# Three-stage float32 kernel: the order of its instructions as lists instead of a planner

## The chip, the cores and the metric

The kernel runs on one core of one Trainium2 chip. The metric is the device time of one execution in microseconds (us); lower is better. The engines are called as the profile calls them: PE is TensorE's matmul, PEld its weight load, DVE is VectorE, ACT is ScalarE, POOL is GpSimd, SP is SyncE, whose queue issues nearly all DMAs.

## The reference

Three stages in float32. A delta-rule attention over 4 batches, 8 heads, 768 steps of 48 features; then a feed-forward layer with squared relu (384 to 2048 to 384); then one whose hidden layer is the maximum of three products (384 to 768 to 384). The 3072 rows are the 4 x 768 tokens.

```python
def _attn_ref(q, k, v, beta):
    k_n = k / (np.linalg.norm(k, axis=-1, keepdims=True) + 1e-06)
    for t in range(S):
        kt, vt, bt = (k_n[:, :, t], v[:, :, t], beta[:, :, t, None])
        y[:, :, t] = np.einsum('bhd,bhde->bhe', q[:, :, t], state)
        v_old = np.einsum('bhde,bhd->bhe', state, kt)
        state = state + bt[:, :, :, None] * np.einsum('bhd,bhe->bhde', kt, vt - v_old)

def _moe_ref(x, w_in, w_out):
    r = np.maximum(x @ w_in, 0.0)
    return (r * r) @ w_out

def _moe2_ref(x, w1, w2, w3, w_out):
    return np.maximum(np.maximum(x @ w1, x @ w2), x @ w3) @ w_out
```

## The kernel before

The tokens are cut into six blocks of 128 steps (index t), 512 tokens each over the four batches. The attention of a block is done in chunks of 64 steps. `gram` (L593) transposes k and q and multiplies keys with keys and queries; `solve` (L687) inverts the small triangular systems, with nearly a hundred short DVE instructions on the tiles `L`, `T`, `F`, `step` and `tmp`, a transposition `L<-G` ahead of them and the transpositions `Tn<-T` and `G<-T` behind them, and small PE products (`Tn,G`, `G`, `G,L`, `L,Tn`); `chain` (L789) carries the state from chunk to chunk, with small PE products (`US,W`, `R,G`, `US,kn`, `W,US`), and leaves the block's output in `xr`. `split` (L922) makes a high and a low part of it, `xh` and `xl`, on ACT and DVE.

The first feed-forward layer (`moe1`, L968) takes a block in 16 slices f of 128 hidden features. `hidden` makes nine matmuls of 512 columns (three of 128 rows each, for three products of high and low parts), three ACT passes (`r`, `r`, `gh`) and one DVE pass (`gl`); `project` makes nine matmuls more with the weights `wo`. In the first block eight slices are done in two halves of 256 columns (`HALF`), and each slice's weights are made there, out of raw float32 words, into a high and a low part: two steps on `word` and `raw` on ACT, four on DVE, and one more on each for the parts (`wih`, `wil` or `wo`). They are written to a DRAM copy (`wod`), from which later blocks load them. The third stage (`maxout`, L1125, and `project2`, L1142) comes at the end, when the first one's outputs of all blocks are there.

All small products are float32 matmuls of 64 columns or fewer; all large ones have 256 to 512 columns and operands in the faster type `F32R`. PE changes between the two kinds: a row of small products is put between rows of large ones.

No engine call goes straight into the program. `_Engine.__getattr__` (L322) records it; `together` (L78) binds calls into one step; `issue` (L292) puts the steps of one of three parts of the kernel into an order and makes the calls, and each engine runs its instructions in that order. The waits between engines are put in by the layer below, from the tiles that the instructions read and write. The order is the `Planner`'s (L54): `add` (L84) notes each step's cost and which steps it depends on, `forward` (L120) lists them by due time on five modelled engines, `backward` (L248) makes new due times out of the result, eight rounds in all, and the best is kept. The due times that it starts from are set along the code in `pl.at`, from constants such as `GL`, `CL`, `GRAM`, `SOLVE` and `CHAIN`; `MIX`, `FULL`, `STAY` and others steer when PE changes kind.

Of the kernel before, what the change touches and what calls it, by code (L numbers as in the profile page):

```python
# [17 lines left out]
WINDOW = 10.24 / 3  # L18
ROUNDS = 8


def _row(t):
    n = 1
    for x in t.shape[1:]:
        n *= x
    return n


def _region(ap):

    t, dims = ap.tensor, list(ap.ap)
    if "DRam" in type(t).__name__:
        return None
    if ap.space == DRAM:
        tile_size = t.shape[-2] * t.shape[-1]
        n = ap.size() // tile_size
        return t.name, 0, 128, ((1 << n) - 1) << (ap.offset // tile_size)
    row = _row(t)
    p0, off = divmod(ap.offset, row)
    if ap.space == PSUM:  # L40
        return t.name, 0, 128, -1
    off += sum(step * (n - 1) for step, n in dims[1:] if step < 0)
    bits = 1
    for step, n in sorted((abs(step), n) for step, n in dims[1:]):
        if step:
            out, done = 0, 0
            while done < n:
                out |= bits << (step * done)
                done += 1
            bits = out  # L50
    return t.name, p0, p0 + (dims[0][0] // row) * (dims[0][1] - 1) + 1, bits << off


class Planner:  # L54

    MIX, FULL, STAY, BURST, URGENT = 0.01, 0.27, 35.22, 19.14, -2.36
    INTO, BACK, RUSH = 0.12, 0.24, 4.896
    HOLD = {"vector": 0.198, "sync": 38.55}
    CHUNK, SUPPLY, AHEAD = 256, 4.0, 128
    EVENT, LANES = 0.065, 8
    PHASE = 67
    LAG = {"tensor": 0.2, "vector": 0.13, "scalar": 0.15, "gpsimd": 0.08, "sync": 0.0}

    def __init__(self, nc):
        self.nc, self.at, self.ops, self.seen, self.joint, self.beside = nc, 0.0, [], {}, None, False  # L70
        self.free, self.first, self.end, self.before_all, self.rush = {}, 0, {}, False, False
        self.flow, self.ticks, self.start = (deque(), False, False, (self.PHASE, -9.0, False)), {}, {}
        self.marks = {}, {}, {}, {}
# [4 lines left out]
    def together(self, beside=False):  # L78

        self.joint, self.beside = len(self.ops), beside  # L80
        yield
        self.joint, self.beside = None, False

    def add(self, engine, call, cost, outs, ins, flow, late, count=0):  # L84
        if self.joint is None or self.joint == len(self.ops):
            self.ops.append([engine, [], 0.0, set(), self.at, any(a.dtype == F32R for a in ins), 0.0, 0.0, self.before_all, self.rush, 0])
        n = len(self.ops) - 1
        op = self.ops[n]
        op[1].append(call)
        op[10] += count  # L90
        op[2] = max(op[2], cost) if self.beside else op[2] + cost
        op[6] += flow
        op[7] = late
        for write, aps in ((False, ins), (True, outs)):
            for ap in aps:
                region = _region(ap)
                if region is None:
                    continue
                name, p0, p1, bits = region
                kept = []  # L100
                for e in self.seen.get(name, ()):
                    m, w, a0, a1, b = e
                    other = bits < 0 and self.ops[m][0] != engine
                    if (write or w or other) and a0 < p1 and p0 < a1 and b & bits:
                        if m != n:
                            op[3].add(m)
                        if write and p0 <= a0 and a1 <= p1 and not b & ~bits:
                            continue
                    kept.append(e)
                kept.append((n, write, p0, p1, bits))  # L110
                self.seen[name] = kept

    def lag(self, m, n):

        e, f = self.ops[m][0], self.ops[n][0]
        if f == "tensor":
            return 0.0 if e == "tensor" else self.LAG[e] + 0.1
        return self.LAG[e]

    def forward(self, at):  # L120

        first, ops = self.first, self.ops
        free, ticks, flow, fill, big, (count, since, thin) = dict(self.free), dict(self.ticks), *self.flow
        flow = deque(flow)
        known, snaps, place, count_of = self.marks
        known, snaps = {e: dict(k) for e, k in known.items()}, {e: list(x) for e, x in snaps.items()}
        place, count_of = dict(place), dict(count_of)
        left, ready, queue, seq = {}, {}, {}, []
        start, end = {}, self.end
        end = dict(end)  # L130
        for n in range(first, len(ops)):
            left[n] = len(self.before[n])

        def there(n):
            t = 0.0
            for m in ops[n][3]:
                t = max(t, end[m] + self.lag(m, n))
            heappush(ready.setdefault(ops[n][0], []), (t, n))

        for n in range(first, len(ops)):  # L140
            if not left[n]:
                there(n)
        todo = len(ops) - first
        while todo:
            best = None
            for e in self.LAG:
                f = free.get(e, 0.0)
                if queue.get(e):
                    t = f
                elif ready.get(e):  # L150
                    t = max(f, ready[e][0][0])
                else:
                    continue
                if best is None or t < best[0]:
                    best = t, e
            t, e = best
            q = queue.setdefault(e, [])
            r = ready.get(e, [])
            hold, later = self.HOLD.get(e, 0.0), []
            while r and r[0][0] <= t + (max(self.RUSH, hold) if hold else 0.0):  # L160
                when, n = heappop(r)
                if when <= t + hold or ops[n][9]:
                    heappush(q, (at[n], n))
                    start[n] = when
                else:
                    later.append((when, n))
            for x in later:
                heappush(r, x)
            n = q[0][1]
            if e == "tensor":  # L170
                while flow and flow[0][0] < t - WINDOW:
                    flow.popleft()
                load = sum(x[1] for x in flow)
                fill = load < (self.FULL if fill else self.MIX)
                kinds = [min((x for x in q if ops[x[1]][5] == f), default=None) for f in (False, True)]
                used = count % self.CHUNK - self.CHUNK * (t - since) / self.SUPPLY
                thin = used > (0 if thin else self.AHEAD)
                if None not in kinds:
                    if fill or thin:
                        n = kinds[True][1]  # L180
                    else:
                        lead = kinds[True][0] - kinds[False][0]
                        if not big:
                            stay = lead > -self.STAY
                        else:
                            stay = lead < self.URGENT and sum(
                                ops[x[1]][2] for x in q if not ops[x[1]][5]
                            ) < self.BURST
                        n = kinds[big if stay else not big][1]
            q.remove((at[n], n))  # L190
            heapify(q)
            t = start[n] = max(t, start[n])
            seq.append(n)
            cost = ops[n][2]
            k, need = known.setdefault(e, {}), {}
            for m in ops[n][3]:
                f, p = ops[m][0], place[m]
                if f == e == "tensor":
                    continue
                r, p = (p % self.LANES, p // self.LANES + 1) if f == "sync" else (f, p)  # L200
                if p > k.get(r, 0):
                    need[r] = max(p, need.get(r, 0))
            for r, p in need.items():
                k[r] = max(p, k.get(r, 0))
                if r != e and r in snaps:
                    for x, y in snaps[r][p - 1].items():
                        k[x] = max(y, k.get(x, 0))
# [40 lines left out]
    def backward(self, end):  # L248
# [5 lines left out]
        def there(n):  # L254
            t = 0.0
# [950 lines left out]
```

## Time and profile before

| | us |
|---|---|
| median of 3 runs | 900.05 (893.88 to 901.16) |
| profiled execution | 900.32 |
| its span, first to last instruction | 898.6 |
| PE busy | 849.2 |
| DVE busy | 550.0 |
| ACT busy | 458.6 |
| POOL busy | 34.6 |

The profile is one execution, with every instruction of every engine. Spans of matmuls overlap, so a PE that is busy all the time may still run at different rates; the count of matmuls in a stretch tells more. The granted clock is a share of PE's full speed. All recorded calls have one line in the profile, L371, so instructions are told apart by operation, tiles and shape.

### The profile page before, as it was taken

The page shows a single profiled execution, that of the slowest core. Times are in us where ns is not written, and L with a number is a line of the kernel's source. Part 1 is how long each engine was busy: PE and PEld are TensorE (multiplying, and loading weights), DVE is VectorE, ACT ScalarE, POOL GpSimd, SP SyncE. Part 2 cuts the span into 40 slices and gives each one's busy share as a digit, 9 for nine tenths or more (in the row PEclk, how much of TensorE's full clock was granted, in tenths as well). Part 3 has the DMA queues.
Part 4 walks back from the last instruction along what each step waited for, and adds up shares of the span by engine and source line. Part 5 has one row for each costly group of instructions (what it writes and reads, how often), then busy time and mean ns, then how long its engine had stood idle before and what let it go on. Part 6 is the DMA issues. An engine that isn't in the chain of part 4 may idle for free.

```text
span 898.6 us, 24256 instructions
## 1 busy us (share of the span) xinstructions
PE 849.2 (95%) x10284; PEld 716.3 (80%) x10284; DVE 550.0 (61%) x1325; ACT 458.6 (51%) x876; POOL 34.6 (4%) x55
## 2 busy tenths in 40 slices
PE   4558999999989999999999999999999999999998
PEld 4447987778768787878878888888888889898987
DVE  5999989879769869969742999223324141413131
ACT  6557877974755575574555899432212121212111
POOL 6000001000100000000000000000000000000000
PEclk9556999999999999999999999999999999999999
DMA  8854584764377466544234777320100000000000
GB/s 209 188 141 110 149 288 124 182 152 129 49 151 176 82 125 144 140 92 109 89 104 138 229 259 232 106 88 1 53 18 37 35 1 36 1 35 1 29 8 36
DMA packets 166893, 96.06 MB, mean 107 GB/s; under 512 B 130560, under 2 KB 146816, under 8 KB 166784
## 3 DMA queue, kind: packets, MB, share of 16 engines
q1 hardware_dynamic: 166272, 94.40, 39.1%
q8 instruction: 81, 1.33, 0.6%
q14 instruction: 28, 0.23, 0.1%
q0 software_dynamic: 512, 0.10, 0.1%
HBM read 79.53 MB, written 14.94 MB: 105 GB/s over the span
## 4 chain that ended last, share of the span: by engine, by line
PE 87%; DVE 5%; ACT 3%; DMA 3%; issue 1%; ACTq 0%; DVEq 0%
PE ps L371 87%; DMA raw<-in_moe_w_in_dram 2%; DVE word L371 1%; DVE T L371 1%; DVE step L371 1%; ACT W L371 1%; ACT G L371 1%; DMA raw<-in_moe_w_out_dram 1%; DVE W L371 1%; DVE F L371 0%; ACT word L371 0%; DVE tmp L371 0%; DMA wo<-wod 0%; ACT US L371 0%; DVE wil L371 0%
## 5 line engine op out<-in xcount | busy, mean ns | idle before, releaser
L371 DVE TENSOR_TENSOR r<-r,ps 128x512 f32<-128x512 f32 x72 | 49.5, 688 | 178.0 <-PE ps L371 176.0
L371 PE MATMUL ps<-gh,wo 128*128 128x512 f32 (+1 forms) x624 | 156.9, 378 | 1.3 <-DMA wo<-wod 0.7
L371 ACT ACTIVATE r<-ps 128x512 f32<-128x512 f32 (+1 forms) x140 | 80.0, 571 | 139.1 <-PE ps L371 132.6
L371 PEld LDWEIGHTS ps<-gh,wo 128*128 128x128 f32 x624 | 110.4, 188 | 22.5 <-DMA wo<-wod 1.1
L371 PE MATMUL ps<-xh,wih 128*128 128x512 f32 (+1 forms) x312 | 120.8, 387 | 0.5 <-ACT r L371 0.5
L371 PE MATMUL ps<-xh,wil 128*128 128x512 f32 (+1 forms) x312 | 117.2, 376 | 0.0
L371 PE MATMUL ps<-xl,wih 128*128 128x512 f32 (+1 forms) x312 | 117.1, 375 | 0.0
L371 DVE TENSOR_TENSOR gl<-r,gh 128x512 fp32r<-128x512 f32 (+1 forms) x104 | 67.3, 647 | 60.1 <-ACT gh L371 55.7
L371 PE MATMUL ps<-gl,wo 128*128 128x512 f32 (+1 forms) x312 | 84.2, 379 | 0.0
L371 PEld LDWEIGHTS ps<-xh,wih 128*128 128x128 f32 x312 | 59.3, 190 | 12.1 <-ACT r L371 0.7
L371 PEld LDWEIGHTS ps<-xl,wih 128*128 128x128 f32 x312 | 59.2, 190 | 10.8
L371 PEld LDWEIGHTS ps<-xh,wil 128*128 128x128 f32 x312 | 59.4, 190 | 9.5
L371 PEld LDWEIGHTS ps<-gl,wo 128*128 128x128 f32 x312 | 56.2, 190 | 11.0 <-DVE gl L371 0.4
L371 ACT ACTIVATE gh<-r 128x512 fp32r<-128x512 f32 (+1 forms) x104 | 62.0, 596 | 3.3 <-PE ps L371 1.3
L371 ACT ACTIVATE r<-r 128x512 f32<-128x512 f32 (+1 forms) x104 | 62.0, 597 | 2.4
L371 ACT ACTIVATE G<-ps 32x256 f32<-32x256 f32 (+3 forms) x116 | 50.3, 448 | 19.0 <-PE ps L371 17.5
L371 PE MATMUL ps<-W 64*64 64x64 f32 (+1 forms) x1664 | 41.2, 244 | 10.1 <-ACT W L371 7.1
L371 PEld LDWEIGHTS ps<-W 64*64 64x64 f32 (+1 forms) x1664 | 35.9, 151 | 17.7 <-ACT W L371 9.1
L371 DVE TENSOR_SCALAR word<-word 128x384 f32<-128x384 f32 (+1 forms) x112 | 41.1, 369 | 9.2 <-ACT word L371 7.9
L371 ACT ACTIVATE m0h<-r 128x512 fp32r<-128x512 f32 x18 | 11.4, 632 | 67.2 <-DVE r L371 67.2
L371 ACT ACTIVATE m1h<-r 128x512 fp32r<-128x512 f32 x18 | 11.4, 632 | 66.6 <-DVE r L371 66.6
L371 ACT ACTIVATE ob<-ps 128x384 f32<-128x384 f32 x24 | 11.8, 491 | 58.3 <-PE ps L371 58.3
(155 smaller groups left out, 1775.1 us busy)
## 6 DMA issues: line engine op xcount, KB each, us to landing
wo<-wod SPq DMA_DIRECT2D x88, 384.0 KB, 3.5
raw<-in_moe_w_out_dram SPq DMA_DIRECT2D x22, 384.0 KB, 4.0
raw<-in_moe_w_dram SPq DMA_DIRECT2D x18, 384.0 KB, 3.6
raw<-in_moe_w_in_dram SPq DMA_DIRECT2D x16, 384.0 KB, 3.8
wod<-wo SPq DMA_DIRECT2D x16, 384.0 KB, 4.5
out_dram<-ob SPq DMA_DIRECT2D x24, 192.0 KB, 1.8
x2d<-raw SPq DMA_DIRECT2D x12, 256.0 KB, 3.5
vn<-in_v_dram SPq DMA_DIRECT2D x14, 192.0 KB, 4.4
```

The source lines that it names most:

```text
L371: self.plan.add(self.name, lambda: fn(*args, **kw), cost, [out], ins, flow, late, count)
```

## The change

The planner, its costs and all due times are gone. A `Recorder` keeps only the recorded calls, in the order in which the code makes them, bound by `together` as before; `ORDER` has three lists of numbers, one for each part, and `issue` makes the calls in their order. The numbers come from a search outside the kernel that moved steps about in each engine's order. The code that makes the calls is the same but for the removed due times, so the steps and their tiles are the same; ACT's program has one more table load.

```diff
-class Planner:
...
-    MIX, FULL, STAY, BURST, URGENT = 0.01, 0.27, 35.22, 19.14, -2.36
...
+ORDER = [
+    """
+30 7 0 27 25 1 24 26 31 5 1096 2 3 1112 15 35 36 1128 37 38 167 49 22 39 50 51 20 52 40 6 53 41 21 42 43 1097 44 45
...
+class Recorder:
+    def __init__(self, nc):
+        self.nc, self.ops, self.joint, self.part = nc, [], None, 0
...
+    def add(self, call):
+        if self.joint is None or self.joint == len(self.ops):
             self.ops.append([])
+        self.ops[-1].append(call)

     def issue(self):
...
-        for k in range(ROUNDS):
-            plan = self.forward(at)
...
-            at = self.backward(plan[2])
...
+        order = [int(n) for n in ORDER[self.part].split()]
+        assert sorted(order) == list(range(len(self.ops)))
+        for n in order:
+            for call in self.ops[n]:
                 call()
+        self.ops, self.part = [], self.part + 1
...
-    GL, CL, G1, DEC, BOOST, SPL, CUT, HALF, G2, LATE, BLOCKS, FIRST, HURRY = -882, 745, 733, 1375, 2244, -595, 6, 8, -527, 228, 3, 0, 0
...
+    CUT, HALF, BLOCKS = 6, 8, 3
```

ACT at the start of the program. `tmp<-ident` is a square root of one element that loads the table with the square root; `word` and `raw` belong to the first weights. Before:

```order
L371 ACT_TABLE_LOAD
L371 ACTIVATE tmp<-ident 128x1
L371 ACTIVATE word_84<-raw_81 128x384
L371 ACTIVATE raw_81<-raw_81 128x384
```

And now, where `tmp<-ident` stands; `st<-st` is the first solve's square root, `W_105` and `G_107` are the first block's keys and products:

```order
L258 ACTIVATE wo_98<-word_84 128x384
L258 ACTIVATE G_107<-ps_93 128x512
L258 ACTIVATE W_105<-ps_90 64x8x64 x2
L258 ACTIVATE word_85<-raw_81 128x384
L258 ACT_TABLE_LOAD
L258 ACTIVATE tmp<-ident 128x1
L258 ACTIVATE st<-st 128x32
```

The one-element square root moved from ACT's first place to behind the first block's evictions. A table load still stands first on ACT, in front of `W_105<-ps_86`, and a second one stands here.

DVE in the first half block of the first feed-forward layer, from the first `gl` to the second `gl`. `L`, `T`, `F`, `step` and `tmp` are those of the second block's solve (t = 1); `F<-F,step` is its first half, `step<-T,F` and `T<-T,step` its second. Before:

```order
L371 TENSOR_TENSOR gl_79<-r_75,gh_77 128x256
L371 TENSOR_TENSOR T<-T,tmp 128x2x4x12
L371 TENSOR_TENSOR step_121<-L,T 128x192
L371 TENSOR_TENSOR tmp<-L,T 128x78
L371 TENSOR_TENSOR F<-F,step_121 128x16x12
L371 TENSOR_TENSOR T<-T,tmp 128x2x3x13
L371 TENSOR_TENSOR step_120<-L,T 128x208
L371 TENSOR_TENSOR F<-F,step_120 128x16x13
L371 TENSOR_TENSOR xl<-xr,xh 128x4x64 x3
L371 TENSOR_TENSOR tmp<-L,T 128x56
L371 TENSOR_TENSOR gl_80<-r_76,gh_78 128x256
L371 TENSOR_TENSOR wo_98<-word_84,wo_98 128x384
```

And now:

```order
L258 TENSOR_TENSOR F<-F,step_121 128x256
L258 TENSOR_TENSOR gl_79<-r_75,gh_77 128x256
L258 TENSOR_TENSOR step_120<-T,F 128x240
L258 TENSOR_TENSOR step_121<-T,F 128x224
L258 TENSOR_TENSOR T<-T,F 128x16x16
L258 TENSOR_TENSOR xl<-xr,xh 128x4x64 x2
L258 TENSOR_TENSOR T<-T,step_120 128x15x16
L258 TENSOR_TENSOR wo_98<-word_84,wo_98 128x384
L258 TENSOR_TENSOR step_120<-T,F 128x208
L258 TENSOR_TENSOR T<-T,step_121 128x14x16
L258 TENSOR_TENSOR gl_80<-r_76,gh_78 128x256
```

The solve has moved forward past the first block's slices: its first half, which was still under way at the first `gl`, is now over there, and its second half stands among the first `gl` and `wo`.

PE where the second block's solve is used. `Tn,G_108`, `G_108`, `G_108,L` and `L,Tn` are its small products, the rest are large matmuls of `hidden` and `project`. Before, in the first block's slices of 512 columns:

```order
L371 MATMUL ps_90<-Tn,G_108 32x32
L371 MATMUL ps_90<-G_108 32x32
L371 MATMUL ps_88<-gh_77,wo_100 128x512 x2
L371 MATMUL ps_86<-gl_79,wo_100 128x512
L371 MATMUL ps_87<-gl_79,wo_100 128x512
L371 MATMUL ps_88<-gl_79,wo_100 128x512
L371 MATMUL ps_86<-gh_78,wo_101 128x512 x2
L371 MATMUL ps_87<-gh_78,wo_101 128x512 x2
L371 MATMUL ps_91<-G_108,L 32x32
L371 MATMUL ps_90<-L,Tn 32x32
```

And now, where the last half slice ends (the pieces of 4x64 columns):

```order
L258 MATMUL ps_90<-Tn,G_108 32x32
L258 MATMUL ps_90<-G_108 32x32
L258 MATMUL ps_89<-xh,wih 128x512
L258 MATMUL ps_89<-xh,wil 128x512
L258 MATMUL ps_89<-xl,wih 128x512
L258 MATMUL ps_86<-gl_80,wo_101 128x4x64
L258 MATMUL ps_87<-gl_80,wo_101 128x4x64
L258 MATMUL ps_88<-gl_80,wo_101 128x4x64
L258 MATMUL ps_86<-gh_77,wo_98 128x512 x2
L258 MATMUL ps_90<-Tn,G_108 32x32
L258 MATMUL ps_90<-G_108 32x32
```

The products of one solve stood in two rows of 64, with nine large matmuls between them. Now the first 64 are in three parts of 32, 16 and 16, with two and eight large ones between these, and 16 large ones stand before the other 64; all of it comes earlier among the large matmuls.

## Rows read from the trace of the kernel before

**Rows 1.** The page: busy time by engine, PE in 40 slices, the instruction queue's packets

```profile
PE 849.2 (95%) x10284; PEld 716.3 (80%) x10284; DVE 550.0 (61%) x1325; ACT 458.6 (51%) x876; POOL 34.6 (4%) x55
...
PE   4558999999989999999999999999999999999998
...
q8 instruction: 81, 1.33, 0.6%
```

**Rows 2.** Stretches: us, busy us (count) of PE, PEld, DVE, ACT, POOL; clock; DMA

```profile
30.00:90.00 60.00, 34.88 (x968) 30.13 (x964) 57.71 (x191) 36.78 (x76) 3.15 (x4) 0.57 0.55 138
...
91.00:150.00 59.00, 57.86 (x712) 52.83 (x702) 55.53 (x154) 47.30 (x109) 1.36 (x2) 1.00 0.63 200
...
100.00:130.00 30.00, 28.88 (x287) 28.11 (x287) 26.98 (x73) 23.67 (x62) 0.00 (x0) 1.00 0.82 269
...
150.00:160.00 10.00, 8.14 (x231) 6.66 (x217) 8.42 (x16) 7.38 (x14) 1.99 (x2) 0.83 0.39 101
...
150.00:190.00 40.00, 36.78 (x1060) 29.13 (x1050) 31.35 (x60) 34.67 (x73) 3.96 (x6) 0.96 0.64 156
...
200.00:220.00 20.00, 20.00 (x90) 16.57 (x89) 19.69 (x82) 9.32 (x15) 0.00 (x0) 1.00 0.47 148
...
245.00:275.00 30.00, 27.21 (x758) 21.34 (x758) 21.39 (x59) 15.00 (x33) 0.00 (x0) 0.94 0.74 144
...
275.00:425.00 150.00, 148.44 (x2729) 120.83 (x2728) 127.77 (x338) 90.16 (x164) 6.34 (x8) 1.00 0.54 124
...
314.38:331.65 17.27, 17.27 (x435) 14.01 (x429) 10.68 (x15) 13.29 (x27) 1.90 (x2) 1.00 0.61 118
...
485.00:895.00 410.00, 410.00 (x1969) 351.97 (x1967) 158.87 (x278) 148.77 (x274) 0.00 (x0) 1.00 0.20 67
```

**Rows 3.** PE's waits by releaser (us, times, longest): from 120 us on; 150 to 190

```profile
PE ps L371 <- issue: 6.7, 6, 1.9
...
PE ps L371 <- issue: 3.0, 2, 1.9
```

**Rows 4.** PE, instructions in order of time (start, us; idle before in brackets), 147 to 262

```profile
147.15 0.73 PE L371 MATMUL ps<-gh,wo 128*128 128x512 f32 x2
...
149.41 0.21 PE L371 MATMUL ps<-G,L 32*32 32x32 f32 x1
...
152.06 0.21 PE L371 MATMUL ps<-G,L 32*32 32x32 f32 x1 [1.86 <-issue]
...
154.08 0.63 PE L371 MATMUL ps<-xl,wih 128*128 128x512 f32 x1
154.51 0.63 PE L371 MATMUL ps<-xh,wih 128*128 128x512 f32 x1
...
261.28 0.34 PE L371 MATMUL ps<-US,W 64*64 64x48 f32 x2 [1.95 <-issue]
```

**Rows 5.** ACT, PE and DVE in order of time, up to 21 us

```profile
0.81 1.28 ACT L371 ACT_TABLE_LOAD   x1 [0.81 <-PEq L1190]
2.10 0.20 ACT L371 ACTIVATE tmp<-ident 128x1 f32<-128x1 f32 x1
...
7.58 1.09 PE L371 MATMUL ps<-ident,kt 128*128 128x128 f32 x4 [7.58 <-DMA kt<-in_k_dram]
...
5.01 0.76 DVE L371 TENSOR_SCALAR word<-word 128x384 f32<-128x384 f32 x2 [2.94 <-ACT word L371]
...
18.47 1.95 DVE L371 STREAM_TRANSPOSE L<-G 128x1024 f32<-128x1024 f32 x1
```

**Rows 6.** DVE and PE in order of time: a first solve's step, the eighth `gl`, a transposition

```profile
45.82 0.40 DVE L371 TENSOR_TENSOR step<-T,F 128x240 f32<-128x240 f32 x1
...
109.38 0.42 DVE L371 TENSOR_TENSOR gl<-r,gh 128x256 fp32r<-128x256 f32 x1
...
111.94 0.28 PE L371 MATMUL ps<-gl,wo 128*128 128x256 f32 x1
...
143.31 2.04 DVE L371 STREAM_TRANSPOSE G<-T 128x1024 f32<-128x1024 f32 x1
```

More of the change, by code (lines that the diff above doesn't have):

```diff
@@ L17 @@
 DRAM = bass.MemoryType.DRAM
[L18 to L51, printed above, removed]
-class Planner:
-    MIX, FULL, STAY, BURST, URGENT = 0.01, 0.27, 35.22, 19.14, -2.36
[L62 to L67, printed above, removed]
+ORDER = [
+    """
[148 rows of a table added]
+""",
+    """
[22 rows of a table added]
+""",
+    """
[22 rows of a table added]
+""",
+]
+class Recorder:
     def __init__(self, nc):
[L70 to L73, printed above, removed]
+        self.nc, self.ops, self.joint, self.part = nc, [], None, 0
         for name in ("tensor", "vector", "scalar", "gpsimd", "sync"):
@@ L77, in together @@
     @contextmanager
-    def together(self, beside=False):
-        self.joint, self.beside = len(self.ops), beside
+    def together(self):
+        self.joint = len(self.ops)
         yield
-        self.joint, self.beside = None, False
-    def add(self, engine, call, cost, outs, ins, flow, late, count=0):
+        self.joint = None
+    def add(self, call):
         if self.joint is None or self.joint == len(self.ops):
[L86 to L207, printed above, removed]
-            place[n] = count_of.get(e, 0) + (e != "sync")
-            count_of[e] = count_of.get(e, 0) + 1
-            if e != "sync":
-                snaps.setdefault(e, []).append(dict(k))
-            if e in ("vector", "scalar"):
-                cost += self.EVENT * max(0, len(need) - 1)
-            if e == "tensor":
-                if ops[n][5] != big:
-                    big = not big
-                    cost += self.BACK if big else self.INTO
-                tick = int(t / WINDOW)
-                if ticks.get(tick - 1, 0.0) < 3060:
-                    cost *= 2
-                issued = ops[n][10] + max(0, len(need) - 1)
-                over = (count + issued) % self.CHUNK
-                if over < count % self.CHUNK:
-                    cost += max(0.0, since + self.SUPPLY - t - cost)
-                    since = t + cost
-                count += issued
-                flow.append((t + cost, ops[n][6]))
-                a, b = t, t + cost
-                while a < b:
-                    tick = int(a / WINDOW + 1e-9)
-                    c = min(b, (tick + 1) * WINDOW)
-                    ticks[tick] = ticks.get(tick, 0.0) + ops[n][6] * (c - a) / cost
-                    a = c
-            if e == "sync":
-                free[e] = t + 0.6
-                free["dma"] = max(t + 1.5, free.get("dma", 0.0)) + cost
-                end[n] = free["dma"] + 0.65
-            else:
-                free[e] = end[n] = t + cost
-                end[n] += ops[n][7]
-            todo -= 1
-            for m in self.after.get(n, ()):
-                left[m] -= 1
-                if not left[m]:
-                    there(m)
-        return seq, start, end, (free, ticks, (flow, fill, big, (count, since, thin)), (known, snaps, place, count_of))
@@ L292, in issue @@
-    def issue(self):
-        first, ops = self.first, self.ops
-        self.after, self.before = {}, {}
-        for n in range(first, len(ops)):
-            self.before[n] = [m for m in ops[n][3] if m >= first]
-            for m in self.before[n]:
-                self.after.setdefault(m, []).append(n)
-        at = {n: n - 1e6 if ops[n][8] else ops[n][4] for n in range(first, len(ops))}
-        best = None
-        for k in range(ROUNDS):
-            plan = self.forward(at)
-            total = max(plan[2][n] for n in at)
-            if best is None or total < best[0]:
-                best = total, plan
-            at = self.backward(plan[2])
-            for n in at:
-                if ops[n][8]:
-                    at[n] = n - 1e6
-        seq, _, self.end, (self.free, self.ticks, self.flow, self.marks) = best[1]
-        for n in seq:
-            for call in ops[n][1]:
+            self.ops.append([])
@@ L368, in record @@
-            flow = 0.0
-            if self.name == "tensor":
-                flow = k * cols / 128 * (1 if ins[0].dtype == F32R or what == "transpose" else 2)
-            self.plan.add(self.name, lambda: fn(*args, **kw), cost, [out], ins, flow, late, count)
+            self.plan.add(lambda: fn(*args, **kw))
         return record
@@ L618, in products @@
             for x in range(n):
-                with pl.together(beside=True):
+                with pl.together():
                     for p0, q0, c0 in ((0, 64, 64), (64, 0, 128)):
@@ L756, in solve @@
         for n in range(NP):
-            with pl.together(beside=True):
+            with pl.together():
                 for p0 in (0, 64):
@@ L765, in solve @@
         pl.scalar.activation(M1[:, 0:NP], pm, AF.Copy)
-        adv(1)
         pa, pb = (a_ring().rearrange("p (n x) -> p n x", n=NP) for c in range(2))
         for n in range(NP):
-            with pl.together(beside=True):
+            with pl.together():
                 for p0 in (0, 64):
@@ L855, in run @@
             for x in range(GP):
-                with pl.together(beside=True):
+                with pl.together():
                     for stage in stages:
@@ L868, in outputs @@
                 for step in range(4):
-                    with pl.together(beside=True):
+                    with pl.together():
                         for q in range(4):
@@ L1018, in project @@
                     )
-        todo = [(f, None, at + 6 * f) for f in range(first, last)]
+        todo = [(f, None) for f in range(first, last)]
         if t == 0:
-            todo[0:HALF] = [(f, c, 3 * (c * HALF + f)) for c in range(2) for f in range(HALF)]
+            todo[0:HALF] = [(f, c) for c in range(2) for f in range(HALF)]
         for n, x in enumerate(todo):
@@ L1027, in moe1 @@
             elif first:
[L1028 removed]
+                project(first - 1, None)
         if last < NF:
```

170 lines of the change are left out of this document (17 added, 153 removed), and 191 rows, old and new, of the table ORDER.

## The prediction

> **What bounds the kernel now.** I read the page from the top, then stretches, then the waits, then single instructions. The page's head [rows 1] gives TensorE (PE) 849.2 of 898.6 us: whatever the new order wins must come out of the other 49 us, or out of stretches in which PE counts as busy but runs slowly. The row of slices places both. PE is short of nine tenths in the first four slices of 22.5 us and in the twelfth (247 to 270 us). Behind the twelfth it is full up to the last.
>
> The stretches [rows 2] split that up. Up to 90 us VectorE (DVE) is the bound: from 30 to 90 us it is busy for 57.71 of 60, while PE has 34.88 at a mean clock of 0.57, so mostly at the lower of its two levels (1.2 of 2.4 GHz). From 91 to 150 both are nearly full (PE 57.86 of 59, DVE 55.53). From 150 to 190 both have holes: PE 36.78 of 40, DVE 31.35. From 245 to 275 PE has 27.21 of 30 at a clock of 0.94. From 485 to 895 PE is busy for 410.00 of 410 us.
>
> A busy PE still hides losses. In 200 to 220 us there are 90 matmuls of 512 columns in 20.00 us, 222 ns each. From 314.38 to 331.65 us PE has no gap either; by its order that stretch holds 45 of them and 384 small float32 matmuls (the row's 435 counts a few that overlap its ends). 45 times 222 ns are 10.0 us, and the other 7.3 us make 19 ns per small one, changes between the two kinds included. By these two rates 150 to 190 us, with 56 large and 1004 small, should take 12.4 + 19.1 = 31.5 us and takes 40: 8.5 too many. 245 to 275 us, with 52 large and 706 small, should take 11.5 + 13.4 = 24.9 us and takes 30: 5.1 too many.
>
> The waits say why [rows 3]. From 120 us on 6.7 us of PE's idle time, in six waits, have no releaser but "issue", 3.0 of them from 150 to 190 us. The two longest, 1.86 and 1.95 us, lie inside runs of small matmuls [rows 4]. Behind the first the 512-column matmuls start 0.43 us apart (154.08, 154.51) where 0.222 is usual: the granted clock has fallen, to 0.83 over those 10 us [rows 2], and some five such starts cost 1.0 us more. I read "issue" here as instructions that come too slowly. The page has 81 instruction packets [rows 1] for 10284 matmuls and 10284 weight loads, about 254 in one packet; small matmuls use up a packet several times as fast as large ones.
>
> **The change, part by part.** No work changes: the same 1325 DVE instructions, and on ScalarE (ACT) 876 and one more. What changes is who stands before whom, so each term is a stretch.
>
> *Before 91 us.* The first two loads of k now stand ahead of the first weight load; PE's first matmul waited 7.58 us for k [rows 5]. ACT in turn does two evictions before its first weight piece, so DVE's first weight step comes later than 5.01 us [rows 5]. Three weight pieces instead of four stand before the first transposition of L, at 18.47 us, some 2.3 us of DVE less. But the second `xl`, on which the first large matmuls rest, keeps its place: DVE's instructions before it, at their distances in this trace, sum to within 0.2 us of what they were. DVE is full on the way, so I take 0, with -2.5 (all of the three pieces' gain) and +2.0 as ends.
>
> *The table load.* ACT's second table load stands right before the square root that the first solve waits for. The trace has one, at the very start: 1.28 us [rows 5]. DVE has a weight step and a mask product to do beside it, so I take +0.5, between 0 (hidden) and +1.3. The Trainium skill ("ScalarE: Activation LUTs", What ACT_TABLE_LOAD costs) adds a drain of about 1380 ns to every switch, 2.66 us in all; here the next ACT instruction starts at 2.10, 0.01 us after the load's end [rows 5], so the trace shows no such drain at that place. By the page the sum would come out up to 1.4 us higher.
>
> *From 91 to 190 us.* Here the order really moves. The second half of the second solve (`step<-T,F`, `T<-T,step`) now stands among the first `gl` and `wo` of the half blocks on DVE; its last transposition, `G<-T` at 143.31 [rows 6], has 8.5 us less DVE work ahead of it, and `Tn<-T` before it 15.0 us less: 33 weight and `gl` instructions have gone behind that. The price: seven `step<-T,F`, six `T<-T,step`, the `T<-T,F`, one `F` and two weight steps now stand ahead of the eighth `gl` that did not, 17 instructions of about the 0.40 us of the first `step<-T,F` [rows 6], 6.3 us at their distances in this trace. What queues behind them on DVE is `wo` and `gl`, and PE's projections wait for those. In this trace the eighth `gl` ends at 109.80 and PE uses it at 111.94 [rows 6]: 2.1 us of slack. DVE's idle time from 100 to 130 us, 30 less 26.98 = 3.0 [rows 2], can take up part. PE is then 1.2 to 4.2 us late there, with only 32 small rows to fill in.
>
> It comes back because the solve's small products now run while PE is still in the second half blocks, and the chain and gram products of the next block are spread over 115 large matmuls before the last of them instead of 65 (counted in PE's order). Of the 8.5 us I expect that to take 7.5, less about 2 of the lateness: -5.5. Ends: all of it and all of DVE's 8.65 idle us between 150 and 190 gone, with the lateness hidden, -11; nothing regained and 4.2 lost, +4.2. I take the middle because it is nearest to the row of issue waits (3.0 idle, 1.0 for the clock, and small matmuls slowed between them).
>
> *From 190 to 275 us.* Two runs of 64 small rows had only four large matmuls between them before the 1.95 us wait; now 11 to 14 large ones separate every such pair there. I take -3.0 of the 5.1, with 0 and -5.1 as ends.
>
> *From 275 to 485 us.* PE is idle for 1.56 us [rows 2] up to 425; -1.2, between 0 and -1.6.
>
> *More changes of kind.* PE's order has 65 runs of small matmuls where it had 61. Nine large ones between two small runs take 149.41 - 147.15 = 2.26 us [rows 4] against 2.00 at 222 ns: 0.26 for each visit, +1.0 for four, 0 if a split run fills a wait.
>
> *From 485 us on* PE has no gap and the order there can win nothing: 0.
>
> The sum is 0 + 0.5 - 5.5 - 3.0 - 1.2 + 1.0 = -8.2 us. The profiled execution took 900.32 us (1.7 more than its span), 0.3 above the median of the runs shown; 900.3 - 8.2 = 892.1, which I round to 892.
>
> **The rivals.** *The idle time stays (898.5).* If "issue" is not a matter of how fast small matmuls use up instructions, spreading them wins nothing there: the 6.7 us of it and the 2 us of lowered clock behind the two longest remain, and of the 15.2 us in the three terms (8.5, 5.1, 1.6) only 6.5 can be won. Half of that, 3.3, against 1.5 for the visits and the table load leaves -1.8. For it speaks that the waits are few, against it that the two long ones lie inside dense small runs. The Trainium skill ("Runtime: NRT & Kernel Launch", Instruction fetch mechanics) says that instructions come in blocks of 256 while the current one executes, and calls the cost of crossing a block mostly hidden; the 254 per packet agree with the first, the 1.86 and 1.95 us speak against the second as long as no other releaser is found.
>
> *Everything comes back (881).* The lateness of `gl` is hidden, and 150 to 190, 245 to 275 and the two idle times reach the clean rates: -11 - 5.1 - 1.6 and -2.5 before 91 us, with the visits costing nothing and 0.5 for the table: -19.7. DVE speaks against the whole of it: 55.53 + 31.35 of the 99 us between 91 and 190 are DVE work [rows 2], in a chain with PE.
>
> *The early solve starves the first block (909).* DVE stays late by the 7.0 us that stand ahead of its twelfth `gl`, PE has 2.1 of slack and nothing to fill in: 4.9 idle. Waits of that length lower the clock, as behind the 1.86 us one; two such falls at 1.1 are 2.2. The small products then meet the block's end as crowded as before, so nothing is won later, and the visits (1.0) and the table (0.5) are paid: +8.6. It decides once PE's idle time between 91 and 150 us, 1.1 now (59.00 - 57.86 [rows 2]), is above 6. DVE's near-full rows there speak for it; against it, that the first block's later weights have slack and that the same DVE work has then left the stretch behind.
>
> **How the numbers follow.** The measurement tells about 1% (9 us) from no change; faster by that is below 891. Chances: the forecast 0.45 (its own range 887 to 897), idle time stays 0.27, everything back 0.18, starved block 0.10. Of the forecast's share about half lies below 891: 0.22 + 0.18 = 0.40 faster. 0.10 slower. The rest, 0.50, is no change within 1%. The range goes from 880, just under the second rival, to 902, above the first rival, and leaves out most of the last.
>
> **What would show it.** Right: PE's issue waits between 145 and 275 us under 2 us in total; no stretch of 10 us there below a clock of 0.95; the split of the second block's input on DVE 4 to 7 us earlier; PE still full from 485 us before the end. Wrong: PE's waits for `gl` or `wo` between 91 and 150 above 6 us; issue waits as long as now in other places; a start of the large matmuls that moves by more than 2.5 us either way; or a gain that lies before 91 us, where I count none.

## The result: 0.8% slower, and the profile after

The changed kernel takes 903.95 us (median of 12 runs, 902.16 to 907.54), the kernel before 897.07 (12 runs, 892.83 to 901.16): ratio 1.0081, 95% interval 1.0064 to 1.0098. It is slower by less than 1%, but the interval leaves out 1. The forecast was 892.0 us, with a range from 880 to 902.

The page of the kernel after: its head, PE, the clock and DVE in 40 slices, the instruction packets [rows 1]:

```profile
PE 862.4 (96%) x10284; PEld 718.1 (80%) x10284; DVE 547.0 (61%) x1325; ACT 458.3 (51%) x877; POOL 34.3 (4%) x55
...
PE   5667999999999999999999999999999999999998
...
PEclk9567999999999999999999999999999999999999
...
q8 instruction: 81, 1.33, 0.6%
```

The same instructions and one more on ACT; the hole in the twelfth slice is gone; PE is busy for 13.2 us more, though its work is the same. A longer busy time for the same matmuls is the first sign that something makes PE slow without making it idle.

The stretches after, columns as in [rows 2]:

```profile
30.00:90.00 60.00, 41.40 (x1082) 33.73 (x1080) 57.70 (x185) 36.51 (x75) 3.16 (x4) 0.67 0.48 122
91.00:150.00 59.00, 57.27 (x797) 51.38 (x786) 56.97 (x150) 50.01 (x115) 3.41 (x4) 1.00 0.74 218
...
150.00:160.00 10.00, 10.00 (x220) 7.53 (x218) 7.22 (x17) 9.23 (x20) 0.00 (x0) 1.00 0.54 167
150.00:190.00 40.00, 39.19 (x937) 30.21 (x936) 28.10 (x54) 34.16 (x73) 1.51 (x3) 1.00 0.55 134
...
245.00:275.00 30.00, 30.00 (x719) 24.17 (x719) 26.89 (x87) 18.10 (x37) 0.00 (x0) 1.00 0.56 114
275.00:425.00 150.00, 150.00 (x2434) 121.94 (x2433) 125.75 (x330) 86.72 (x157) 6.28 (x8) 1.00 0.50 116
425.00:485.00 60.00, 59.16 (x1330) 45.50 (x1329) 22.17 (x39) 30.37 (x55) 1.90 (x2) 1.00 0.39 119
485.00:895.00 410.00, 410.00 (x1908) 351.82 (x1907) 158.51 (x279) 150.62 (x276) 0.00 (x0) 1.00 0.20 68
```

PE's holes between 150 and 425 us are filled and the clock stays at its upper level. And PE's waits after, from 120 us on [rows 3]:

```profile
PE ps L258 <- issue: 1.0, 2, 0.8
PE ps L258 <- DVE W L258: 0.8, 1, 0.8
PE ps L258 <- ACT r L258: 0.5, 1, 0.5
```

"issue" has fallen from 6.7 us to 1.0. All that the prediction wanted gone is gone, and the kernel is slower. What came instead shows in no idle time; it shows where single instructions start. PE after, in order of time (start, us), from one run of small products between two large matmuls:

```profile
436.44 0.32 PE L258 MATMUL ps<-W,US 128*32 128x64 f32 x8
436.69 0.21 PE L258 MATMUL ps<-Tn,G 32*32 32x32 f32 x1
436.69 0.21 PE L258 MATMUL ps<-G 32*32 32x32 f32 x1
...
436.88 0.19 PE L258 MATMUL ps<-Tn,G 32*32 32x32 f32 x1
436.89 0.19 PE L258 MATMUL ps<-G 32*32 32x32 f32 x1
437.01 0.43 PE L258 MATMUL ps<-W,US 128*32 128x64 f32 x16
437.37 0.21 PE L258 MATMUL ps<-Tn,G 32*32 32x32 f32 x1
...
437.88 0.19 PE L258 MATMUL ps<-G 32*32 32x32 f32 x1
438.00 0.32 PE L258 MATMUL ps<-W,US 128*32 128x64 f32 x8
438.25 0.21 PE L258 MATMUL ps<-Tn,G 32*32 32x32 f32 x1
...
439.06 0.72 PE L258 MATMUL ps<-gh,wo 128*128 128x512 f32 x2
```

Inside one kind the 32-row products start 0.01 us apart. From the last of them to the next `ps<-W,US` it is 0.12 us (436.89 to 437.01; 437.88 to 438.00), and sixteen `ps<-W,US` at 0.014 us take 0.22 of the 0.36 us to the next 32-row product (437.01 to 437.37): 0.14 more. Each change of operand shape costs that, with no wait recorded, because the modelled ends of the matmuls (0.19 us and more) reach over the gap. The lists alternate the kinds of the outputs and of a solve, nine changes in this one run; the planner had kept each kind together but for 11 changes in all. The Trainium skill ("TensorEngine Tiling (Array Packing)", Key Properties) says that a change of tiling mode, not merely of tile, drains TensorE. These rows agree with a pause at such a change and put a price on it; that the pause is a drain they do not show. The prediction did not use that rule.

**An account of PE.** I took the starts of all 10284 matmuls and set against the distance to the next one the pace of its kind: 0.227 us for 512 columns, 0.120 for 256, 0.0146 for a small one of 64 rows, 0.0140 for the outputs (`W,US`), 0.0094 for 32 rows. What is over at a change goes to the change (out of 32 rows 0.111, out of 64 rows or the outputs 0.133, out of a large one 0.09, and 0.11 at the first large one after small ones: the medians of the two traces). What is then over 0.15 us is a wait. So a *visit* (a run of small products between large ones) costs 0.33, a *change* inside it 0.11 to 0.13. From the first large matmul on, us, one profiled execution each:

| kernel (its order) | that run | visits | cost | changes | cost | waits | rest |
|---|---|---|---|---|---|---|---|
| before | 900.32 | 60 | 19.9 | 11 | 1.4 | 13.5 | -0.7 |
| before again | 897.13 | 60 | 19.9 | 11 | 1.4 | 11.1 | -1.4 |
| first part of before | 897.04 | 60 | 19.9 | 11 | 1.4 | 13.0 | -1.3 |
| after | 902.16 | 74 | 23.7 | 66 | 8.4 | 6.3 | -0.2 |
| after again | 904.75 | 74 | 23.7 | 66 | 8.4 | 8.4 | -0.1 |
| first part of after | 904.24 | 74 | 23.7 | 66 | 8.4 | 6.8 | -0.1 |
| regrouped | 897.85 | 74 | 23.8 | 14 | 1.8 | 7.6 | -0.1 |
| before alternating | 910.47 | 60 | 19.8 | 121 | 15.9 | 8.2 | 0.5 |
| more visits | 906.96 | 103 | 34.0 | 11 | 1.4 | 6.4 | 0.6 |
| fewer visits | 896.78 | 60 | 19.9 | 16 | 2.0 | 10.4 | -0.6 |
| fewer visits, late before | 893.69 | 61 | 20.2 | 13 | 1.6 | 8.3 | -0.8 |

Between the first two traces: waits -7.2, visits +3.8, changes +7.0, rest +0.5, and the first large matmul 2.3 us earlier (91.27 to 88.98) with 0.1 less work ahead of it, -2.2: +1.9, where the spans differ by 1.8 (898.6 to 900.4).

### The profile page after: what moved, and what is told of

Same layout as the page of the kernel before. It is cut to its first block, busy times and chain, and to the rows that moved or that the text cites. A ratio compares the mean times of both kernels' runs of the same rounds, so it can differ in the third digit from the quotient of the medians.

```text
span 900.4 us, 24173 instructions
## 1 busy us (share of the span) xinstructions
PE 862.4 (96%) x10284; PEld 718.1 (80%) x10284; DVE 547.0 (61%) x1325; ACT 458.3 (51%) x877; POOL 34.3 (4%) x55
## 4 chain that ended last, share of the span: by engine, by line
PE 89%; DVE 4%; ACT 4%; DMA 1%; issue 1%; SPq 0%; ACTq 0%; DVEq 0%
PE ps L258 89%; DVE word L258 1%; ACT G L258 1%; DMA raw<-in_moe_w_out_dram 1%; DVE step L258 1%; ACT W L258 1%; DVE T L258 0%; DVE W L258 0%; DMA kt<-in_k_dram 0%; ACT raw L258 0%; ACT wih L258 0%; ACT word L258 0%; ACT r L258 0%; ACT US L258 0%; DVE F L258 0%
## 5 line engine op out<-in xcount | busy, mean ns | idle before, releaser
L258 PE MATMUL ps<-gh,wo 128*128 128x512 f32 (+1 forms) x624 | 163.7, 378 | 0.0
L258 ACT ACTIVATE G<-ps 32x256 f32<-32x256 f32 (+3 forms) x116 | 50.9, 448 | 23.8 <-PE ps L258 22.2
L258 PE MATMUL ps<-W 64*64 64x64 f32 (+1 forms) x1664 | 49.2, 241 | 11.5 <-ACT W L258 10.8
L258 PEld LDWEIGHTS ps<-W 64*64 64x64 f32 (+1 forms) x1664 | 39.7, 145 | 21.7 <-ACT W L258 13.1
L258 DVE TENSOR_TENSOR W<-ps,mask 64x512 f32<-64x512 f32 x48 | 33.0, 687 | 21.0 <-PE ps L258 20.5
L258 ACT ACTIVATE m1h<-r 128x512 fp32r<-128x512 f32 x18 | 11.4, 632 | 66.6 <-DVE r L258 66.6
L258 ACT ACTIVATE m0h<-r 128x512 fp32r<-128x512 f32 x18 | 11.4, 632 | 60.9 <-DVE r L258 60.9
```

Of the source, the lines that this page charges most:

```text
L258: self.plan.add(lambda: fn(*args, **kw))
```

## The experiments

The theories: 1, changes of operand shape; 2, TensorE waits there for its instructions; 3, it waits for DVE and ACT. All kernels below are the changed kernel with other lists.

**Which part loses.** One list comes from the other kernel (the order of the kernel before, written as lists, is its program instruction by instruction):

```diff
-ORDER = [after_1, after_2, after_3]
+ORDER = [before_1, after_2, after_3]   # h1
+ORDER = [after_1, before_2, before_3]  # h2
```

> The lists of the changed kernel in the second and third part (weights of the second network, the large matmuls of the last blocks and all of the second network), and in the first part the order of the kernel before, written as a list. If the loss lies in the first part, as the small products there let expect, the time is that of the kernel before, 897 us, within 1.5. If the later parts lose (the prediction gave them 0), it is up to 904 us.

> The other half: the list of the changed kernel in the first part, the order of the kernel before in the second and third. Loss in the first part: 904 us, within 1.5. Loss in the later parts: 897 us.

Measured: 897.89 us (1.0000 of before, 0.9986 to 1.0013) and 903.58 (1.0069, 1.0052 to 1.0086). The whole loss lies in the first part, up to some 485 us.

**Regrouped.** PE's order inside its runs of small products; the pattern, from one of them (`ps<-W` has 64 rows, `W,US` are the outputs):

```diff
-ps_93<-W_105,US_109 32x64 x8
 ps_90<-W_106 64x64
 ps_91<-W_106 64x64
...
-ps_93<-W_105,US_109 32x64 x16
 ps_90<-W_106 64x64
 ps_91<-W_106 64x64
...
-ps_93<-W_105,US_109 32x64 x8
+ps_93<-W_105,US_109 32x64 x32
```

> The changed kernel, with TensorE's order altered only inside its runs of small products: between two large matmuls, products of one operand shape (64 rows, 32 rows, or the outputs' 128 rows by 32 columns) stand together, where the lists alternate them. It removes 52 of 66 changes between small shapes; every other engine keeps its order, and nothing moves past a large matmul. Theory 1 (each change of shape costs 0.11 to 0.13 us of TensorE, and the lists added 54 of them): 6 us faster than the changed kernel, about 897.5 us, 0.99 to 1.005 of the kernel before; from 430 to 480 us the excess over 16 ns a product is gone. Theory 2 (TensorE waits there for its instructions, because the lists put the small products closer together): the same number of instructions in the same stretch, so no change, 902 to 905 us. Theory 3 (the loss is in waits for VectorE or ScalarE): no change or slower, since a product may now stand ahead of one that is ready.

Measured: 897.01 us (12 runs), 0.9997 of before, 0.9984 to 1.0010. Theory 1 alone gives that. PE, the run shown above, in the regrouped kernel:

```profile
435.75 0.99 PE L258 MATMUL ps<-W,US 128*32 128x64 f32 x56
436.67 0.21 PE L258 MATMUL ps<-Tn,G 32*32 32x32 f32 x1
...
437.24 0.19 PE L258 MATMUL ps<-G 32*32 32x32 f32 x1
437.36 0.50 PE L258 MATMUL ps<-gh,wo 128*128 128x512 f32 x1
```

The same 120 products take 437.36 - 435.75 = 1.61 us; before the regrouping 439.06 - 436.44 = 2.62. Eight changes fewer, 1.01 us: 0.126 each. The instructions come, if anything, closer together, so theory 2 falls for this loss, and theory 3 with it.

**The cost doubled.** In the kernel before, for example:

```diff
+ps_92<-W_106,US_109 32x64 x4
 ps_91<-W_105 64x64
 ps_90<-W_105 64x64
 ps_91<-W_105 64x64
 ps_90<-W_105 64x64
+ps_92<-W_106,US_109 32x64 x4
```

> The suspected cost doubled, in the kernel before: its own order, but inside each run of small products between two large matmuls the operand shapes alternate wherever the dependencies allow it. Runs of small products stay 60, changes of shape between small products go from 11 to 121; no large matmul and no other engine's instruction is moved. Theory 1 (0.11 to 0.13 us for each change): 110 x 0.125 = 13.7 us slower, about 911 us, and the stretches from 100 to 490 us carry it, one piece at each change. Theory 2 (instruction supply) and theory 3 (waits for VectorE and ScalarE): the same instructions at the same density, within 2 us of 897.

Measured: 910.37 us, 1.0140 of before (1.0114 to 1.0166): 13.1 us for 110 changes, 0.12 each. By the table the changes took 14.5 us more and the waits some 4 less.

**The price of a visit.** In the kernel before, a group of large matmuls goes into the middle of a run:

```diff
-ps_92<-W_105,US_110 32x64 x32
+ps_92<-W_105,US_110 32x64 x16
 ps_89<-xh,wih 128x256
 ps_89<-xh,wil 128x256
 ps_89<-xl,wih 128x256
+ps_92<-W_105,US_110 32x64 x16
```

> The price of a visit taken by itself, in the kernel before: in 43 of its 60 runs of small products the next group of large matmuls is moved up into the middle of the run, so that 103 runs are left; changes between small shapes stay 11, and no other engine's order is touched. Theory 1 (0.09 us into the small shape and 0.13 out of it, whether anything waits or not): 43 x 0.225 = 9.7 us slower, 907 us. Rival (a large matmul inside a run covers a wait that would stand there otherwise, as the joined runs of the earlier kernel show from the other side): its 11 to 14 us of waits fall by as much as a part of that, and it ends between 899 and 905 us.

Measured: 909.22 us (4 runs), 1.0144 (1.0099 to 1.0189), so 9 to 17 us more; that is above both forecasts, but theory 1's 9.7 us lies inside the interval. By the table 43 visits cost 14.1 us, 0.33 each, and 6.1 of the 12.5 us of waits that the three executions of the order before have on average are gone. Both are true, then: a visit is dearer than theory 1 had it, and it covers waits. PE's waits in this kernel, 91 to 500 us, against 6.7 of "issue" before [rows 3]:

```profile
PE ps L258 <- ACT r L258: 1.6, 2, 1.3
PE ps L258 <- issue: 1.4, 2, 0.8
```

So "issue" does go where small products are thinned out by large ones, as the prediction read it.

**Fewer visits.** From the regrouped order:

```diff
+ps_89<-xh,wih 128x256
+ps_89<-xh,wil 128x256
+ps_89<-xl,wih 128x256
 ps_92<-W_105,US_110 32x64 x8
 ps_93<-W_105,US_110 32x64 x4
 ps_92<-W_105,US_110 32x64 x24
-ps_89<-xh,wih 128x256
-ps_89<-xh,wil 128x256
-ps_89<-xl,wih 128x256
```

> The regrouped kernel, and 14 of its 74 runs of small products joined to a neighbour: where only one to three large matmuls (0.21 to 0.68 us) stand between two runs, these go behind the second run or ahead of the first, so that 60 runs are left, as in the kernel before. Theory 1 (a visit costs one change in and one out, 0.09 + 0.13 us): 14 x 0.225 = 3.1 us faster than the regrouped kernel, 894 us. Rival (the large matmuls between the runs cover the time in which VectorE or ScalarE makes the next small product's input, so the joined run waits instead): no change, 897 us, with waits in the trace as long as the changes saved.

Measured: 896.81 us, 1.0002 (0.9987 to 1.0016), the same as the regrouped kernel: the rival. Fourteen visits gave back 3.9 us and the waits rose from 7.6 to 10.4. Where a product's input is not ready, a visit of large matmuls and a wait are two ways to spend the same time.

**The two orders spliced.** The numbers count the steps of a first part's list; each piece leaves out what stands already:

```diff
+c2 = before[:1572] + regrouped[:3096] + before
+c1 = regrouped[:603] + c2
+c3 = before[:1860] + regrouped[:3096] + before
+c4 = fewer_visits[:3096] + before
```

> One order from pieces, each where its stretch has the smaller excess: the changed kernel's up to about 76 us, the order of the kernel before from there to about 192 us, the regrouped order to about 400 us, the order of the kernel before to the end of the first part; 62 runs of small products, 13 changes between small shapes. If the excess of a stretch belongs to its order, the excess after the first large matmul is 6.5 + 9 + 4.5 = 20 us against 24 in the kernel before, and the start is 1 to 2 us earlier: 891 to 893 us. If the lead of one piece is lost in the next (the next piece waits for VectorE or a transfer at the place where it always did), 896 to 898 us.

> The same splice without its first piece: the order of the kernel before from the start. Its distance from the splice is the worth of the changed kernel's start (k, q loads and the first products, a second load of ScalarE's function table of 1.28 us at 18 us). If the start carries its lead of 1 to 2 us through to the end, this kernel is so much slower than the splice; if the lead is eaten by waits behind it, the same within 0.7 us.

Measured: 900.61 us (1.0046, 1.0030 to 1.0062) and 899.27 (1.0024, 1.0011 to 1.0038). Both expectations failed: outside the seam (where two pieces meet) at about 192 us the pieces keep about their excess, but that seam costs more than they win. PE's waits there, 180 to 210 us, and DVE in order of time, in the splice with the changed kernel's start:

```profile
PE ps L258 <- DVE raw L258: 3.3, 1, 3.3
PE ps L258 <- issue: 1.3, 1, 1.3
...
196.71 1.25 DVE L258 STREAM_TRANSPOSE W<-kt 128x1024 f32<-128x1024 f32 x1 [4.02 <-DMA kt<-in_k_dram]
...
198.34 0.69 DVE L258 COPY raw<-ps 128x512 f32<-128x512 f32 x1
```

DVE copies the finished block out late there (`raw<-ps`), because the regrouped order puts a transposition of k ahead of that copy, and DVE stands for 4.02 us until k is loaded. The order before has this copy at 195.11 and transposes k only at 227.7. The wait is for a load, then, not for DVE's own work. The new start won nothing by itself: with it the splice was no faster.

> The order with fewer visits up to about 400 us, and from there to the end of the first part the order of the kernel before; 61 runs of small products, 13 changes between small shapes. The seam at 400 us stood without a wait in both splices before this one (3.6 us of excess behind it, as in the kernel before, against 6.3 in the order with fewer visits). If the excess goes with the order of a stretch: 1.8 to 2.6 us faster than the order with fewer visits, 894.2 to 895.0 us, and so faster than the kernel before by 2 to 3 us. If the last stretch waits for what the lists had put later, 897 us.

> The order of the kernel before up to about 235 us, the regrouped order from there to 400 us, then that of the kernel before again. The splices that changed over at 192 us lost 5.7 us at that seam; here the two orders have done the same work on TensorE and ScalarE and 1.5 us of VectorE's apart. If that loss was the seam's, this kernel has the waits of the kernel before up to 235 us and the regrouped order's smaller excess between 235 and 400 us: 1 to 2.5 us faster than the kernel before, 895 to 896.5 us. If it was the regrouped order that can't follow the earlier one, 900 us as the splices.

Measured: 895.01 us (0.9991, 0.9979 to 1.0003) and 900.12 (1.0048, 1.0032 to 1.0064). The later seam holds, and this order has the lowest ratio of all, 0.9991 against the changed kernel's 1.0081, some 8 us; from the kernel before it can't be told apart. The other seam is no better at 235 us. PE's waits there, 225 to 270 us, and DVE in order of time; this trace is of the slowest execution, 906.10 us, so its waits are longer than is usual for this order:

```profile
PE ps L258 <- DVE R L258: 4.1, 1, 4.1
PE ps L258 <- DVE W L258: 3.3, 2, 2.7
...
241.34 1.25 DVE L258 STREAM_TRANSPOSE W<-kt 128x1024 f32<-128x1024 f32 x1 [5.97 <-DMA qt<-in_q_dram]
242.50 0.52 DVE L258 TENSOR_TENSOR R<-vn,ps 128x384 f32<-128x384 f32 x1
```

An equal amount of work done is no sign that two orders fit together: in these traces of the earlier seams DVE stands in front of a load of k or q, with the result that PE needs next queued behind it.

**Chance or order.** Both kernels were profiled once more.

> The kernel before, profiled once more. The execution that the prediction was made from took 900.3 us, and the runs of the same kernel have a median of 897.1. If what the prediction took back (the issue waits of 1.9 us at 152 and 2.0 us at 261, and the slow small products at 147 and 247) belongs to the order, it stands again at the same places and the large work from 490 us on begins as late as before. If it was chance of that one execution, some of it is missing, and the run is 3 to 6 us shorter from 145 to 275 us.

> The changed kernel once more, for a second profile. Theory 1: its waits on TensorE after the first large matmul are again near 6 us against 11 to 14 in the kernel before, and its changes of shape cost 24.5 us against 14.6: 902 to 905 us. If the loss had been chance of the first comparison, 897 us.

Measured: 897.13 us (one run), and 904.40 (1.0073, 1.0052 to 1.0095), as theory 1 has it, though with waits of 8.4 us and not near 6. PE's waits in the second execution of the kernel before, 91 to 490 us:

```profile
PE ps L371 <- issue: 5.4, 8, 1.4
PE ps L371 <- ACT r L371: 1.1, 1, 1.1
PE ps L371 <- DMA wo<-wod: 0.7, 1, 0.7
```

Most of the waits belong to the order, but not their length: the execution that the prediction was made from had 13.5 us of them, this one 11.1. For the same matmuls from 145 to 275 us this one takes 3.6 us less, so part of what the prediction hoped to win was chance. That first execution stood 3.25 us above its kernel's median of 12 runs, and the profiled one after 1.79 below its own: 1.84 + 3.25 + 1.79 = 6.9, the difference of the medians.

What "issue" is can be settled from the same traces, which hold the times of the 81 instruction packets. All 22 "issue" waits between 91 and 490 us in the three executions of the old order end 1.2 to 1.6 us after a packet has landed: PE waits there for its instructions, as the prediction read it. A packet is in transfer for 1.0 us in the median; the one before the wait of 1.86 us took 3.1 (147.55 to 150.67). At the same place the second execution has no "issue" wait, and the one with the first part of before has one of 1.05, so much of that wait was chance.

## Why the prediction was wrong

Its mechanism held in part: the "issue" waits are late instructions, and they went. "What would show it" came out nearly whole in the first two traces: issue waits between 145 and 275 us 0.2 (under 2); no 10 us there below a clock of 0.95; PE full from 485 us on. The split of the second block's input on DVE starts at 185.09, where it was 188.67: 3.6 us earlier, a little under the 4 to 7; but in the second executions it is 187.15 and 185.35, 1.8 earlier. One sign of being wrong showed too, a gain before 91 us. None of the signs looked at how PE's own pace changes, so none could catch what decided.

**The step that failed** is the term *More changes of kind*, "+1.0 for four". Measured: +10.8, of it 3.8 for fourteen visits and 7.0 for 55 changes. Three errors lie in it. Only changes between large and small were counted, as if all small matmuls were one kind. The count was 65 against 61 where the traces have 74 against 60: the nine that are missing are as many as the new order has ahead of 150 us, so it is probably these that were left out. And the price of 0.26 was read inside the large ones, so that the 0.13 out of the small shape was not in it. The rates of 222 and 19 ns "by these two rates" hid the rest: 19 ns holds the changes at the density of the old order, and was used for the new one.

**A second step that failed** is the -5.5 from 91 to 190 us. Its "8.5 too many" counts every matmul that is not large at 19 ns, but 32 of the 1004 are transpositions with 128 columns, which are neither kind. PE before, eight of them:

```profile
184.60 0.66 PE L371 MATMUL ps<-ident,qt 128*128 128x128 f32 x4
185.09 0.60 PE L371 MATMUL ps<-ident,kt 128*128 128x128 f32 x4
185.62 0.26 PE L371 MATMUL ps<-US,W 64*64 64x48 f32 x2
```

They start some 0.12 us apart, so the 32 make about 3 us of the 8.5. By the account only 5.0 us from 150 to 190 were waits and lowered clock. The waits in all fell by 7.2 us where the three terms had 9.7. That the term of the changes, 9.8 us short, nearly makes up the whole miss of 10.0 between the two traces is luck in part: the start of the large matmuls (below) gave back what the waits did not.

By stretches of equal matmul work, the excess (time over the pace of each kind: visits, changes, waits and rest together) before and after:

- *Before 91 us*: forecast 0, measured -2.2. L's first transposition came at 16.23 instead of 18.47 [rows 5], the 2.3 us counted. That the gain at the large matmuls is the order's is not shown: with the same instructions on DVE and ACT they start at 88.93 to 91.27 us in five executions of the old order and at 88.98 to 90.36 in five of the new one. What the second table load cost of its +0.5 is lost in that. One row says how the table load fell out; ACT after:

```profile
17.89 1.28 ACT L258 ACT_TABLE_LOAD   x1
19.18 0.20 ACT L258 ACTIVATE tmp<-ident 128x1 f32<-128x1 f32 x1
```


  It ends without a drain, 0.01 us ahead of the next instruction, as at the start. The Trainium skill's 2.66 us ("ScalarE: Activation LUTs", What ACT_TABLE_LOAD costs) again don't show.
- *91 to 185 us*: forecast -5.5, measured 9.1 to 11.4, +2.3. The early solve was spread over the half blocks as described, and paid some 0.3 for each place it was spread to: 27 visits instead of 14, +3.7, against 1.3 us of waits won, or 2.6 with the wait that ends at 189.74, which the prediction counted in this term. The lateness of `gl` cost little: PE is idle for 59.00 - 57.27 = 1.7 us between 91 and 150.
- *185 to about 267 us*: forecast -3.0, measured 10.0 to 6.0, -4.0; waits alone -5.2. Right for this execution: its waits there are 6.1, those of the two others of the old order 4.2 and 5.5.
- *to about 424 us*: forecast -1.2, measured 10.4 to 9.3, -1.1. Right in the sum, by luck: waits -1.8 and four visits fewer -1.2, against 15 more changes, +1.9.
- *to about 492 us*: nothing forecast beyond the visits, measured 4.7 to 11.6, +6.9: 4.1 for 33 more changes, 1.3 for four visits, 1.0 for a wait. PE had no idle time there before, so I read no further; a full PE was taken for a PE that can't get slower.
- *From 485 us on*: 0, as forecast.

The base was another, smaller error: that execution stood 3.25 us above the median. Its waits, 13.5 us, are 0.5 and 2.4 more than in the two other executions of its order. "0.3 above the median" rested on three runs.

Of the rivals, "the idle time stays" falls, since issue waits went. "Everything comes back" was near with its -5.1 and -1.6 (waits -5.2 and -1.8), far off with its -11 (waits -1.3), and had the changes at nothing. "The early solve starves the first block" is decided by its own sign (1.7 us, not 6). The case that came true, slower through PE's own pace, was none of them. How far a still better order could win stays open; no order tried was measurably faster than the planner's.

## What to carry to other kernels

Before a reordering is priced, count the changes of operand shape in each engine's new order, small against small too, and price them from the distance of starts, not from idle time: on TensorE 0.11 to 0.13 us each. Where an engine is full, its pace can still fall; an order that is chosen by its waits alone can buy them off with changes. And take the base of a small forecast from several executions: those of the kernel before went from 892.83 to 901.16 us, more than the effect.

## What the runs showed of the hardware

- A change of operand shape on TensorE costs 0.111 us out of 32x32 and 0.132 to 0.133 out of 64x64 or 128x32 (medians; 110 added changes measured 0.12 each, 52 removed ones 6.9 us). Between 64x64 and 64x48 no cost shows (starts 0.007 to 0.038 us apart in the median, where products of one kind go at 0.015 on average).
- The first large matmul after small ones starts 0.34 us ahead of the second, instead of 0.227.
- "issue" waits of TensorE are waits for instruction packets: in all 14 traces the 47 of them between 91 and 490 us end 1.2 to 1.6 us after a packet has landed. They are 5.4 to 6.7 us in three executions of the old order and 0.3 to 1.5 in three of the new one, with the same 81 packets, so it is not the number of packets that sets them. They are 2.4 where the old order's small products alternate and 1.4 where it has more visits. An estimate: a packet holds some 127 small products with their weight loads (20568 in 81 packets), at 0.0146 us used up in 1.9 us, where a packet is in transfer for 1.0 us and the waiting instruction starts 1.2 to 1.6 us after that.
